# First products of the experts in seven half-size forms, and float64 weights turned to float32 beforehand

## The chip, the cores and the metric

One Trainium2 chip, one of its cores. The metric is device time in microseconds (us) of one execution. Engines: PE (TensorE, matrix products into PSUM banks), DVE (VectorE), ACT (ScalarE), POOL (GpSimd), SP (SyncE, which issues the DMAs).

## The reference, cut to what matters

An attention layer (2 batches of 768 tokens, 8 heads) gives x, 1536 tokens of 512 values. On x works a layer of eight experts, on its result a gated last layer. All is float32, but the last layer's weights and the lengths come as eight-byte numbers.

```python
logits = x @ w_gate
P = np.exp(logits - logits.max())
for _ in range(8):
    P /= P.sum(1, keepdims=True) + 1e-09
    P /= P.sum(0, keepdims=True) + 1e-09
    P *= N / E
for e in range(E):                      # 8 experts, w1[e] 512 x 1024, w2[e] 1024 x 512
    h = np.maximum(x @ w1[e], 0.0)      # the first products
    out += P[:, e:e + 1] * (h @ w2[e])  # the second products
# last layer: w_gate, w_val 512 x 1536 and w_out 1536 x 512, all float64
gate = 1.0 / (1.0 + np.exp(-(x @ w_gate)))
y = gate * (x @ w_val) @ w_out
```

## The kernel before

Matrix products run as three float32r passes on operands that are split in two parts, x = high + low: high x high, low x high, high x low (`product`, lines 283 to 285). So every operand exists twice: `xh`, `xl` (x with its 512 values on the partitions, tokens as columns), `wh`, `wl` (weights), `hh`, `hl` (the hidden layer). A split is an ACT copy for the high part and a subtraction for the low one, on POOL for weights (line 203) and on DVE for results in a bank (line 317).

The work comes in visits. A visit is a quarter of an expert (256 of its 1024 hidden values), or a sixth of the last layer, over all its chunks of tokens. `unit_first` makes the first products of a chunk: for each of 2 blocks of 128 hidden values 12 products (4 blocks of the contraction, 3 passes) into one bank, then ACT's Relu (316) and DVE's `hl` (317). `unit_second` makes the second products one unit later: per block of 128 tokens 6 products of 512 columns, which DVE adds to `acc` with the gate as factor (359). Chunks have 4 blocks of tokens (512 columns) from the second expert on. The first expert is done in two batches of 768 tokens with chunks of 3 blocks (384 columns): the first batch beside the second batch's attention, the second beside the gate. The gate's logits, then eight rounds of row and column sums (`gate_steps`), are issued step by step between the products of that second batch; a column sum is a PE product with ones (961), and a chain of eight DVE operations (lines 967 to 974 and 952 to 955) makes what the next one reads.

All queues are in the order in which the code issues (`manual_schedule`); `Paced` spreads side work over ticks, one after each product group. While a visit runs, the weights of the next are split (`split_steps`); its last step issues the load that refills the raw buffer (`load`, on SP). From the last expert visit on, each visit's next weights are float64, loaded as pairs of words and taken apart by `split_double`: seven DVE operations of 1024 columns, one on ACT, one on POOL for each of three parts. In the last layer `turn_y` transposes the experts' sum into `xh`, `xl`, paced over the last expert visit and the first of the last layer.

## Time and profile before

| | us |
|---|---|
| median of 3 runs | 1505.39 (1503.59 to 1505.69) |
| span of the profiled execution | 1504.86 |
| PE busy / DVE busy / ACT busy / POOL busy | 1485.4 / 740.1 / 346.6 / 241.0 |
| chain that ended last: PE / DVE | 95% / 3% |
| first products, 512 columns | 3 x 960 |
| first products, 384 columns | 3 x 128 |
| second products, 512 columns | 3 x 912 |

The profile is one execution of the program. Busy PE time is modelled and products overlap in it, so the distance between the starts of products tells more than their durations. Waits are inferred from semaphores; a wait that stands in a row in brackets is idle time of that row's engine just ahead of it. Lines (L283) are those of the kernel printed above.

### The profile page before, as it was taken

The page shows a single profiled execution, that of the slowest core. Times are in us where ns is not written, and L with a number is a line of the kernel's source. Part 1 is how long each engine was busy: PE and PEld are TensorE (multiplying, and loading weights), DVE is VectorE, ACT ScalarE, POOL GpSimd, SP SyncE. Part 2 cuts the span into 40 slices and gives each one's busy share as a digit, 9 for nine tenths or more (in the row PEclk, how much of TensorE's full clock was granted, in tenths as well). Part 3 has the DMA queues.
Part 4 walks back from the last instruction along what each step waited for, and adds up shares of the span by engine and source line. Part 5 has one row for each costly group of instructions (what it writes and reads, how often), then busy time and mean ns, then how long its engine had stood idle before and what let it go on. Part 6 is the DMA issues. An engine that isn't in the chain of part 4 may idle for free.

```text
span 1504.9 us, 17508 instructions
## 1 busy us (share of the span) xinstructions
PE 1485.4 (99%) x7091; PEld 1233.7 (82%) x7091; DVE 740.1 (49%) x1257; ACT 346.6 (23%) x638; POOL 241.0 (16%) x254
## 2 busy tenths in 40 slices
PE   8999998999999999999999999999999999999998
PEld 6889877888888888888888888888888788888887
DVE  5654436553443434343434444343454676786663
ACT  5754322211112111111111111111111232222121
POOL 4322102211111112111211111121211100110010
PEclk9999999999999999999999999999999999999999
DMA  8421101101000101100010100011011101211102
GB/s 192 95 69 39 29 30 56 43 28 43 29 29 29 42 29 30 41 29 28 28 43 29 42 29 28 28 36 35 30 41 57 56 28 57 84 56 57 56 0 84
DMA packets 75525, 68.30 MB, mean 45 GB/s; under 512 B 40112, under 2 KB 57520, under 8 KB 75440
## 3 DMA queue, kind: packets, MB, share of 16 engines
q1 hardware_dynamic: 75152, 67.14, 14.9%
q8 instruction: 57, 0.93, 0.3%
q14 instruction: 28, 0.23, 0.0%
q10 hardware_dynamic: 288, 0.00, 0.0%
HBM read 63.98 MB, written 3.15 MB: 45 GB/s over the span
## 4 chain that ended last, share of the span: by engine, by line
PE 95%; DVE 3%; ACT 1%; issue 1%; DMA 0%; DVEq 0%; ACTq 0%; POOL 0%; POOLq 0%
PE bank L283 30%; PE bank L285 29%; PE bank L284 29%; PE bank L652 1%; PE bank L682 1%; PE bank L700 1%; PE bank L696 1%; PE bank L507 0%; ACT e L669 0%; DVE acc L359 0%; PE bank L518 0%; DVE qT L622 0%; DMA lens<-in_n_local_dram 0%; PE bank L1003 0%; DVE e L664 0%
## 5 line engine op out<-in xcount | busy, mean ns | idle before, releaser
L283 PE MATMUL bank<-xh,wh 128*128 128x512 f32 (+1 forms) x1088 | 421.0, 387 | 2.8 <-issue 2.8
L284 PE MATMUL bank<-xl,wh 128*128 128x512 f32 (+1 forms) x1088 | 418.8, 385 | 0.3 <-DVE xl L1008 0.2
L285 PE MATMUL bank<-xh,wl 128*128 128x512 f32 (+1 forms) x1088 | 418.8, 385 | 0.0
L283 PE MATMUL bank<-wh,hh 128*128 128x512 f32 x912 | 359.5, 394 | 0.0
L285 PE MATMUL bank<-wh,hl 128*128 128x512 f32 x912 | 355.9, 390 | 0.0
L284 PE MATMUL bank<-wl,hh 128*128 128x512 f32 x912 | 355.5, 390 | 0.0
L317 DVE SCALAR_TENSOR_TENSOR hl<-bank,hh 128x512 fp32r<-128x512 f32 (+1 forms) x200 | 134.0, 670 | 432.0 <-ACT hh L316 432.0
L359 DVE SCALAR_TENSOR_TENSOR acc<-bank,gate,acc 128x512 f32<-128x512 f32 x336 | 252.1, 750 | 145.2 <-PE bank L285 140.8
L316 ACT ACTIVATE hh<-bank 128x512 fp32r<-128x512 f32 (+1 forms) x200 | 116.2, 581 | 821.9 <-PE bank L285 815.7
L203 POOL TENSOR_TENSOR wl<-raw,wh 128x512 fp32r<-128x512 f32 x136 | 174.0, 1300 | 790.1 <-ACT wh L201 788.3
L283 PEld LDWEIGHTS bank<-xh,wh 128*128 128x128 f32 x1088 | 205.2, 189 | 42.3 <-issue 3.0
L284 PEld LDWEIGHTS bank<-xl,wh 128*128 128x128 f32 x1088 | 205.5, 189 | 39.9 <-DVE xl L1008 1.2
L285 PEld LDWEIGHTS bank<-xh,wl 128*128 128x128 f32 x1088 | 205.5, 189 | 38.5
L285 PEld LDWEIGHTS bank<-wh,hl 128*128 128x128 f32 x912 | 171.3, 188 | 36.5
L283 PEld LDWEIGHTS bank<-wh,hh 128*128 128x128 f32 x912 | 171.7, 188 | 35.6
L284 PEld LDWEIGHTS bank<-wl,hh 128*128 128x128 f32 x912 | 171.5, 188 | 34.3
L274 POOL TENSOR_TENSOR wl<-raw 128x1024 fp32r<-128x1024 f32 x18 | 34.1, 1896 | 282.3 <-PE bank L285 139.7
L201 ACT ACTIVATE wh<-raw 128x512 fp32r<-128x512 f32 x136 | 78.6, 623 | 0.0
L331 DVE TENSOR_TENSOR z<-bank,sg 128x512 f32<-128x512 f32 x36 | 24.9, 690 | 66.0 <-PE bank L285 66.0
L669 ACT ACTIVATE e<-e,mn 128x256 f32<-128x256 f32 (+1 forms) x96 | 41.9, 483 | 50.0 <-DVE mn L664 49.8
L332 ACT ACTIVATE hh<-z 128x512 fp32r<-128x512 f32 x36 | 22.7, 632 | 88.0 <-DVE z L331 88.0
L333 DVE TENSOR_TENSOR hl<-z,hh 128x512 fp32r<-128x512 f32 x36 | 27.6, 768 | 25.1 <-ACT hh L332 25.1
(112 smaller groups left out, 768.7 us busy)
## 6 DMA issues: line engine op xcount, KB each, us to landing
raw<-in_moe_w_dram SPq DMA_DIRECT2D x68, 512.0 KB, 3.5
raw<-in_moe_w_val_dram SPq DMA_DIRECT2D x6, 1024.0 KB, 5.2
raw<-in_moe_w_gate_dram SPq DMA_DIRECT2D x6, 1024.0 KB, 5.2
raw<-in_moe_w_out_dram SPq DMA_DIRECT2D x6, 1024.0 KB, 4.9
out_dram<-o SPq DMA_DIRECT2D x12, 256.0 KB, 2.0
qr<-in_q_dram SPq DMA_DIRECT2D x14, 192.0 KB, 4.0
kr<-in_k_dram SPq DMA_DIRECT2D x14, 192.0 KB, 4.2
vo<-in_v_dram SPq DMA_DIRECT2D x14, 192.0 KB, 3.3
```

Source lines behind the costliest of these rows:

```text
L201: steps.append(lambda r=r, h=h: nc.scalar.activation(out=h, in_=r, func=AF.Copy))
L203: lambda r=r, h=h, lo=lo: nc.gpsimd.tensor_tensor(out=lo, in0=r, in1=h.bitcast(F32), op=ALU.subtract)
L274: nc.gpsimd.tensor_tensor(out=lo, in0=low, in1=high, op=ALU.mult)
L283: nc.tensor.matmul(out=ps, lhsT=ah, rhs=bh, start=(i == 0), stop=False)
L284: nc.tensor.matmul(out=ps, lhsT=ah, rhs=bl, start=False, stop=False)
L285: nc.tensor.matmul(out=ps, lhsT=al, rhs=bh, start=False, stop=(i == n - 1))
L316: nc.scalar.activation(out=hh[hid][:, f, :m], in_=ps, func=AF.Relu)
L317: nc.vector.scalar_tensor_tensor(out=hl[hid][:, f, :m], in0=ps, scalar=0.0, in1=hh[hid][:, f, :m].bitcast(F32), op0=ALU.max, op1=ALU.subtract,
L331: nc.vector.tensor_tensor(out=z, in0=ps, in1=sg, op=ALU.mult)
L333: nc.vector.tensor_tensor(out=hl[hid][:, f, :m], in0=z, in1=hh[hid][:, f, :m].bitcast(F32), op=ALU.subtract,)
L359: nc.vector.scalar_tensor_tensor(out=a, in0=ps, scalar=gate[:, t, e : e + 1], in1=a, op0=ALU.mult, op1=ALU.add,)
L669: nc.scalar.activation(out=e[:, j, lo:KW], in_=e[:, j, lo:KW], func=AF.Exp, scale=-1.0, bias=mn[:, j : j + 1],)
```

## The change

From the second expert on a visit is of a new kind (`fast`). Contraction (512), hidden values (256) and tokens (768 of a batch) are each cut in two halves, and the eight half-size products that make a visit's first products of one batch are replaced by seven products of combinations, by the Strassen scheme in Winograd's form. `pair` runs them for a batch: each form is 6 PE products of 384 columns; a form may add to what an earlier one left in its bank, after ACT has copied that (`copied`) and before DVE adds a copy (`summed`). One second product, or two, stands between forms.

- The weights' seven forms: four POOL operations on 256 columns (`sum_steps`) and seven splits of 256 columns on ACT and POOL (`form_step`), for the next visit beside this one. All visits share one set of forms.
- The tokens' forms: `trans_steps` makes them once per batch, 8 DVE operations and 4 splits on 768 columns, issued beside the gate (`other`). One block of `xh`, `xl` is overwritten by its form.
- The hidden layer has three buffers, not two.
- The last layer's weights: `double_steps` fetches float64 in 36 half-pieces, turns each to float32 on DVE (6 operations on 512 columns), ACT (1) and POOL (2), and stores it to DRAM (`glw`), step by step over 26 of the 28 visits. In the last layer they are loaded and split as other weights are, by ACT and POOL.
- The turning of y: the first chunk's transposes stand among the last six second products of the experts, the others in the first visit of the last layer.

```diff
+    hh3 = const.tile([P, HID, 2, C], F32R, name="hh3")
+    glw = [dram.tile([P, 4 * FQ], F32, name=f"glw{i}") for i in range(3 * NFF)]
...
-                dict(kind="moe", e=e, f=f, chunks=chunks, slot=1 - len(visits) % 2, load=True)
+            visits.append(dict(kind="fast", e=e, f=f, slot=1 - len(visits) % 2, load=True))
...
+    def split_one(r, h, lo):
+        nc.scalar.activation(out=h, in_=r, func=AF.Copy)
+        nc.gpsimd.tensor_tensor(out=lo, in0=r, in1=h.bitcast(F32), op=ALU.subtract)
...
+    def sum_steps(n):
+        a, (s1, s2, s3, s4) = w1_blocks(n), sums()
+        for out, x, y, op in (
+            (s1, a[1, 0], a[1, 1], ALU.add), (s2, s1, a[0, 0], ALU.subtract),
+            (s4, a[0, 1], s2, ALU.subtract), (s3, a[0, 0], a[1, 0], ALU.subtract),
+        ):
+            yield lambda out=out, x=x, y=y, op=op: nc.gpsimd.tensor_tensor(
+                out=out, in0=x, in1=y, op=op
+            )
+    def form_step(n, i):
+        a, (s1, s2, s3, s4) = w1_blocks(n), sums()
+        src = (a[0, 0], s1, s2, s4, s3, a[0, 1], a[1, 1])[i]
+        h, lo = form(i)
+        split_one(src, tall(h), tall(lo))
...
+        return [
+            fetch, no_tick, no_tick, rest, first_a, first_b, keep, kept, scaled, whole, no_tick,
+            store,
+        ]
...
+        run(0, x, block(0, 0))
+        copied(0, x)
+        slots(0)
+        run(1, z, trans(0))
+        copied(1, z)
+        slots(1)
+        seconds(1)
+        run(2, x, trans(1), start=False)
+        copied(2, x)
+        slots(2)
+        seconds(1)
+        run(3, z, block(1, 1), start=False)
+        summed(t_hid, 0, z, snap[:, 2])
+        slots(3)
+        seconds(1)
+        run(4, x, trans(2), start=False)
+        summed(t_hid, 1, x, snap[:, 1])
+        slots(4)
+        seconds(1)
+        run(5, y, block(1, 0))
+        o_hid = next_hid()
+        summed(o_hid, 0, y, snap[:, 0])
+        slots(5)
+        seconds(2)
+        run(6, x, block(0, 1), start=False)
+        hidden(o_hid, 1, x)
...
+        return [
+            whole(r11, 0, 0), whole(r12, 0, 1), whole(r22, 1, 1), whole(r21, 1, 0),
+            less(r11, r12, r11), put(r11, th[:, 0, :, b, :], tl[:, 0, :, b, :]),
+            less(r12, r22, r12), put(r12, th[:, 2, :, b, :], tl[:, 2, :, b, :]),
+            less(r22, r22, r11), put(r22, th[:, 1, :, b, :], tl[:, 1, :, b, :]),
+            less(r21, r21, r22), put(r21, *block(0, 1)),
+        ]
...
+    trans = [x for b in range(B) for x in trans_steps(b)]
     side = Paced(gate_steps(), 5 * CB * NQ - 2)
-    for n in range(NB0, 2 * NB0):
-        run_visit(n, side.tick)
+    other = Paced([no_tick] * 6 + trans[:-1], 5 * CB * (NQ - 1))
...
+    for n in range(NB0, F0 - 1):
+        run_visit(n, both, split_steps(n + 1))
+    other.finish()
...
+    ahead = [*sum_steps(F0), *(lambda i=i: form_step(F0, i) for i in range(4)), *second_steps(F0)]
+    run_visit(n, side.tick, ahead)
     side.finish()
+    trans[-1]()
+    for i in range(4, 7):
+        form_step(F0, i)
+    load(visits[F0]["raw"])
...
+    doubles = Paced(double_steps(), 26 * (last - F0 - 1))
```

Three places show how the queues change. The first is DVE in the gate stage, around one chain of the gate (`csum` to the second `gate` row); `acc` and `hl` are the first expert's, `work` holds the tokens' combinations. Before:

```order
L349 COPY acc_5355<-bank_68 128x512
L317 SCALAR_TENSOR_TENSOR hl_79<-bank_63,hh_77 128x384
L317 SCALAR_TENSOR_TENSOR hl_79<-bank_64,hh_77 128x384
L967 TENSOR_REDUCE csum<-bank_70 128x8
L970 TENSOR_SCALAR csum<-csum 128x8
L973 RECIPROCAL csum<-csum 128x8
L974 TENSOR_TENSOR gate<-gate,csum 128x96
L952 TENSOR_REDUCE rsum<-gate 128x12
L953 TENSOR_SCALAR rsum<-rsum 128x12
L954 RECIPROCAL rsum<-rsum 128x12
L955 TENSOR_TENSOR gate<-gate,rsum 128x96
L351 TENSOR_TENSOR acc_5355<-bank_66,acc_5355 128x512
```

In the changed kernel:

```order
L1122 TENSOR_TENSOR work<-work 128x768
L427 COPY acc_5373<-bank_68 128x512
L393 SCALAR_TENSOR_TENSOR hl_77<-bank_63,hh_76 128x384
L1122 TENSOR_TENSOR work<-work 128x768
L393 SCALAR_TENSOR_TENSOR hl_77<-bank_64,hh_76 128x384
L1204 TENSOR_REDUCE csum<-bank_70 128x8
L1207 TENSOR_SCALAR csum<-csum 128x8
L1210 RECIPROCAL csum<-csum 128x8
L1211 TENSOR_TENSOR gate<-gate,csum 128x96
L1189 TENSOR_REDUCE rsum<-gate 128x12
L1190 TENSOR_SCALAR rsum<-rsum 128x12
L1191 RECIPROCAL rsum<-rsum 128x12
```

Two combinations of 768 columns now stand ahead of the chain, and others between the next ones.

The second is SP at the load that follows the first fast visit's split; `raw` is a buffer of raw weights, `work` here the buffer of float64 words, `glw` the store in DRAM. Before:

```order
L182 DMA raw_88<-in_moe_w_dram 128x4x256
L182 DMA raw_88<-in_moe_w_dram 128x2x512
L182 DMA raw_89<-in_moe_w_dram 128x4x256
L182 DMA raw_89<-in_moe_w_dram 128x2x512
L182 DMA raw_88<-in_moe_w_dram 128x4x256
L182 DMA raw_88<-in_moe_w_dram 128x2x512
L182 DMA raw_89<-in_moe_w_dram 128x4x256
L182 DMA raw_89<-in_moe_w_dram 128x2x512
```

In the changed kernel:

```order
L175 DMA raw_86<-in_moe_w_dram 128x4x256
L175 DMA raw_86<-in_moe_w_dram 128x2x512
L297 DMA work<-in_moe_w_gate_dram 128x2x512
L340 DMA glw_90<-work 128x512
L297 DMA work<-in_moe_w_gate_dram 128x2x512
L175 DMA raw_87<-in_moe_w_dram 128x4x256
L175 DMA raw_87<-in_moe_w_dram 128x2x512
L340 DMA glw_90<-work 128x512
L297 DMA work<-in_moe_w_val_dram 128x2x512
```

The conversion's first fetch stands behind that load, and each further fetch behind the store of the one before it, with weight loads between.

The third is DVE in the expert visits, around one unit of first products before and part of one batch's forms after; `kept` holds the copies of banks and the sums. Before:

```order
L317 SCALAR_TENSOR_TENSOR hl_78<-bank_63,hh_76 128x512
L317 SCALAR_TENSOR_TENSOR hl_78<-bank_64,hh_76 128x512
L359 SCALAR_TENSOR_TENSOR acc_5355<-bank_70,gate,acc_5355 128x512
L359 SCALAR_TENSOR_TENSOR acc_5355<-bank_67,gate,acc_5355 128x512
L359 SCALAR_TENSOR_TENSOR acc_5355<-bank_68,gate,acc_5355 128x512
L359 SCALAR_TENSOR_TENSOR acc_5355<-bank_69,gate,acc_5355 128x512
L317 SCALAR_TENSOR_TENSOR hl_79<-bank_65,hh_77 128x512
L317 SCALAR_TENSOR_TENSOR hl_79<-bank_66,hh_77 128x512
L359 SCALAR_TENSOR_TENSOR acc_75<-bank_70,gate,acc_75 128x512
L359 SCALAR_TENSOR_TENSOR acc_75<-bank_67,gate,acc_75 128x512
```

In the changed kernel:

```order
L539 TENSOR_TENSOR kept<-bank_66,kept 128x384
L437 SCALAR_TENSOR_TENSOR acc_75<-bank_68,gate,acc_75 128x512
L531 SCALAR_TENSOR_TENSOR hl_77<-kept,hh_76 128x384
L301 TENSOR_SCALAR work<-work 128x512
L539 TENSOR_TENSOR kept<-bank_64,kept 128x384
L308 TENSOR_SCALAR work<-work 128x512
L437 SCALAR_TENSOR_TENSOR acc_75<-bank_69,gate,acc_75 128x512
L531 SCALAR_TENSOR_TENSOR hl_77<-kept,hh_76 128x384
L539 TENSOR_TENSOR kept<-bank_65,kept 128x384
L314 SCALAR_TENSOR_TENSOR work<-work 128x512
L437 SCALAR_TENSOR_TENSOR acc_75<-bank_70,gate,acc_75 128x512
L531 SCALAR_TENSOR_TENSOR hl_77<-kept,hh_76 128x384
```

The additions into `kept`, on which later forms wait, now stand among the second products' sums and the conversion's operations on `work`.

## Rows read from the trace of the kernel before

**Rows 1.** The page's parts 1 and 2: busy us, share, instructions; then clock by slice.

```profile
PE 1485.4 (99%) x7091; PEld 1233.7 (82%) x7091; DVE 740.1 (49%) x1257; ACT 346.6 (23%) x638; POOL 241.0 (16%) x254
...
PEclk9999999999999999999999999999999999999999
```

**Rows 2.** The page's part 4: the chain that ended last, share of the span by engine.

```profile
PE 95%; DVE 3%; ACT 1%; issue 1%; DMA 0%; DVEq 0%; ACTq 0%; POOL 0%; POOLq 0%
```

**Rows 3.** Busy us of each engine by window (instructions), granted clock, DMA share, GB/s.

```profile
220.00:272.00 52.00, 47.35 (x229) 42.57 (x228) 31.51 (x82) 9.60 (x19) 10.68 (x9) 0.93 0.13 41
280.00:1180.00 900.00, 900.00 (x3972) 745.25 (x3971) 378.96 (x521) 157.32 (x276) 140.15 (x109) 1.00 0.10 33
```

**Rows 4.** PE in order of time: start us, us, line, operation, out<-in, shape.

```profile
379.91 0.39 PE L283 MATMUL bank<-wh,hh 128*128 128x512 f32 x1
...
383.76 0.39 PE L285 MATMUL bank<-wh,hl 128*128 128x512 f32 x1
```

**Rows 5.** PE in order of time, 384 columns.

```profile
247.12 0.33 PE L283 MATMUL bank<-xh,wh 128*128 128x384 f32 x1
...
248.19 0.33 PE L283 MATMUL bank<-xh,wh 128*128 128x384 f32 x1
...
251.14 0.33 PE L285 MATMUL bank<-xh,wl 128*128 128x384 f32 x1
```

**Rows 6.** DVE by line and shape: out<-in, count, busy us, mean ns, idle before, releaser.

```profile
L359 DVE SCALAR_TENSOR_TENSOR acc<-bank,gate,acc 128x512 f32<-128x512 f32 x336 | 252.1, 750 | 145.2 <-PE bank L285 140.8
...
L333 DVE TENSOR_TENSOR hl<-z,hh 128x512 fp32r<-128x512 f32 x36 | 27.6, 768 | 25.1 <-ACT hh L332 25.1
...
L253 DVE SCALAR_TENSOR_TENSOR tmp<-raw,tmp 128x1024 int32<-128x1024 int32 x18 | 22.0, 1222 | 0.4
...
L317 DVE SCALAR_TENSOR_TENSOR hl<-bank,hh 128x384 fp32r<-128x384 f32 x32 | 17.8, 558 | 56.1 <-ACT hh L316 56.1
```

**Rows 7.** ACT and POOL by line and shape, the whole span.

```profile
L316 ACT ACTIVATE hh<-bank 128x384 fp32r<-128x384 f32 x32 | 15.7, 492 | 75.9 <-PE bank L285 69.8 <-DVE rsum L953 6.0
...
L203 POOL TENSOR_TENSOR wl<-raw,wh 128x512 fp32r<-128x512 f32 x136 | 174.0, 1300 | 790.1 <-ACT wh L201 788.3 <-issue 1.0 <-DVE qT L622 0.7
...
L606 POOL TENSOR_TENSOR bm<-bm,msk 128x256 f32<-128x256 f32 x6 | 4.4, 726 | 0.2
```

**Rows 8.** The page's part 6: DMA issues, KB each, us to landing.

```profile
raw<-in_moe_w_dram SPq DMA_DIRECT2D x68, 512.0 KB, 3.5
raw<-in_moe_w_val_dram SPq DMA_DIRECT2D x6, 1024.0 KB, 5.2
```

**Rows 9.** PE in order of time around a wait of the gate stage.

```profile
257.59 0.46 PE L961 MATMUL bank<-gate,ones 128*128 128x96 f32 x2 [1.78 <-DVE gate L955]
...
259.49 0.52 PE L285 MATMUL bank<-xh,wl 128*128 128x384 f32 x1
...
262.05 0.52 PE L284 MATMUL bank<-xl,wh 128*128 128x384 f32 x1
```

**Rows 10.** DVE in order of time: two chains of the gate stage.

```profile
246.57 0.25 DVE L967 TENSOR_REDUCE csum<-bank 128x8 f32<-128x96 f32 x1
...
246.85 0.17 DVE L970 TENSOR_SCALAR csum<-csum 128x8 f32<-128x8 f32 x1
...
248.34 0.26 DVE L955 TENSOR_TENSOR gate<-gate,rsum 128x96 f32<-128x96 f32 x1
...
254.01 1.15 DVE L970 TENSOR_SCALAR csum<-csum 128x8 f32<-128x8 f32 x1
```

**Rows 11.** DVE by line, 220 to 272 us.

```profile
L974 DVE TENSOR_TENSOR gate<-gate,csum 128x96 f32<-128x96 f32 x7 | 3.4, 482 | 0.2
...
L970 DVE TENSOR_SCALAR csum<-csum 128x8 f32<-128x8 f32 x7 | 3.2, 457 | 0.2
...
L953 DVE TENSOR_SCALAR rsum<-rsum 128x12 f32<-128x12 f32 x7 | 1.9, 266 | 0.2
```

**Rows 12.** Waits from 1150 to 1200 us: us in total, times, longest.

```profile
PE bank L1003 <- DVE xl L1008: 1.5, 2, 1.2
```

More of the change, by code (lines that the diff above doesn't have):

```diff
@@ L25 @@
 FILL = 4
-HID = 2
+HID = 3
 PACE = 13
@@ L187, in load, with piece, load_piece, split_halves @@
             )
+    def piece(i):
+        return raw[i // 2 % 2][:, i % 2 * 4 * FQ : (i % 2 + 1) * 4 * FQ]
+    def load_piece(i):
+        if i < 3 * NFF:
+            nc.sync.dma_start(out=piece(i), in_=glw[i])
+    def split_one(r, h, lo):
+        nc.scalar.activation(out=h, in_=r, func=AF.Copy)
+        nc.gpsimd.tensor_tensor(out=lo, in0=r, in1=h.bitcast(F32), op=ALU.subtract)
+    def split_halves(r, h, lo):
+        for half in range(2):
+            cols = slice(half * 2 * FQ, (half + 1) * 2 * FQ)
+            yield lambda cols=cols: split_one(r[:, cols], h[:, cols], lo[:, cols])
+    def second_steps(n):
+        vis = visits[n]
+        r = raw[vis["raw"]][:, 4 * FQ : 8 * FQ]
+        yield from split_halves(r, wh[vis["slot"]][1], wl[vis["slot"]][1])
     def split_steps(n):
-        if n >= len(visits) or not visits[n]["load"]:
-            return []
         vis = visits[n]
@@ L380, in turn, with run_visit @@
             turns.pop(0)[1]()
-    def run_visit(n, tick, after=None):
+    def run_visit(n, tick, ahead):
         chunks = visits[n]["chunks"]
-        steps = split_steps(n + 1)
         per = chunks[0][1] + (2 if visits[n]["kind"] == "moe" else 4)
-        ahead = Paced(steps, per * (len(chunks) - 1) * (12 if n == last else PACE) // 12)
+        ahead = Paced(ahead, per * (len(chunks) - 1) * PACE // 12)
         side = tick
@@ new lines, in run_fast, with before, after @@
+    def run_fast(n, side):
+        fast = n < last
+        ahead = list(sum_steps(n + 1)) if fast else []
+        seconds = list(second_steps(n + 1)) if fast else []
+        def before(i):
+            side()
+            if i is None and ahead:
+                ahead.pop(0)()
+        def after(i):
+            side()
+            if not fast:
+                if i is not None:
+                    state["after"](i)
+            elif i is None:
+                if seconds:
+                    seconds.pop(0)()
+            elif i > 0:
+                form_step(n + 1, i - 1)
+        pair(n, 0, before)
+        for step in ahead:
+            step()
+        pair(n, 1, after)
+        if fast:
+            form_step(n + 1, 6)
+            load(visits[n + 1]["raw"])
```

440 lines of the change are left out of this document (275 added, 165 removed).

## The prediction

> **What bounds the kernel now.** The page's first parts come first: PE is busy for 1485.4 of 1504.9 us, its granted clock is full in every slice, DVE and POOL for 49% and 16% [rows 1]. The chain that ended last is 95% PE [rows 2]. So a PE product that is removed shortens the span, and added work on another engine costs only where PE waits for it. Two windows show both kinds of place. From 280 to 1180 us (the experts from the second on) PE never idles; from 220 to 272 us (the gate's normalisation, beside the first expert's second batch) PE is busy for 47.35 of 52 us at a mean clock of 0.93 [rows 3].
>
> PE's busy time is modelled, so products are priced by the distance between their starts. Eighteen 512-column products in a row start from 379.91 to 383.76 us: 3.85 / 17 = 226.5 ns each [rows 4]. Eighteen 384-column ones start from 248.19 to 251.14 us: 2.95 / 17 = 173.5 ns [rows 5]. That is 0.766 for 0.75 of the columns: about 13 ns of each product don't shrink.
>
> **First products: the term that pays.** A visit (a quarter of an expert, 28 of them from the second expert on) has 3 chunks of 2 blocks with 12 first products each, 72 of 512 columns: 72 x 0.2265 = 16.31 us. Changed, it has 2 batches of 7 forms with 6 products each, 84 of 384 columns: 84 x 0.1735 = 14.57 us. The gain is 1.74 us a visit, 28 x 1.74 = 48.6 us. By columns alone (one eighth less) it would be 28 x 2.04 = 57 us; the fixed 13 ns of 336 additional products take the rest. The stretch of 24 that follows a change of width gives 174.8 ns (247.12 to 251.14) [rows 5], hence 45.6 us; I take 48, with 45 as its lower bound. PE gets no other work: its instruction list is longer by exactly these 336 products with their loads.
>
> Section "Wait — 56ns, not 53.3ns?" of the Trainium skill's page "TensorE: Matmul & The Clock Gate" puts the start-to-start distance at columns by 2.4 GHz plus about 2.5 ns. By that the gain would be 28 x (72 x 215.8 - 84 x 162.5 ns) = 53 us, an estimate from the page; the trace has larger fixed parts, so the rows decide.
>
> **The seven forms' other work in a visit pair.** A pair (one batch) lasts 42 x 0.1735 + 36 x 0.2265 = 15.4 us on PE. DVE gets 6 sums into `acc` at 0.75, 3 additions and 4 `hl` at 0.56, and 0.69 of a float64 half-piece (36 in 26 visits; six operations of at most 0.61, half of the dearest 1024-column row): 4.5 + 3.9 + 2.5 = 10.9 us. ACT gets 7 copies or Relus at 0.49 and not as much again for forms: under 7 us. POOL gets 2 sums and 3.5 forms at 0.73, one half at 1.30 and the conversion's two operations at 1.30: 7.1 us [rows 6, 7]. All fit in 15.4.
>
> In order, too, there is room. Form 2 accumulates on the bank that ACT copied after form 0: between them lie form 1 and one second product, 1.04 + 1.36 = 2.4 us, for a 0.49 us copy. Form 6 needs DVE's addition of form 4: form 5 and two second products lie between, 3.8 us, for 0.56. I cost steady pairs at nothing; PE's own second products cover them. A float64 fetch that comes behind two weight loads on SP can hold DVE up: three transfers of 512 KB land after about 3.5 + 2 x (5.2 - 3.5) = 6.9 us [rows 8], and the operation that waits is placed some 6 us after its fetch. This falls on about six of 36 fetches, mostly inside the slack: +1 us, bounds 0 and 8.
>
> **First fast visit.** Here the load that SP must issue ahead of the first fetch waits for POOL, which has 4 sums and 7 forms (8.0 us), two halves (2.6) and one 768-column subtraction (about 1.95, 1.5 x 1.30) to do, 12.6 us from about where the last chunk begins, 8.3 us ahead of the visit [rows 7]. So the load is issued 4.3 us into the pair and the fetch lands near 11.2. DVE waits for it with the addition of form 4 queued behind. This pair has only three second products pending, so PE reaches form 6 at 6 x 1.04 + 3 x 1.36 = 10.3 us and gets its bank at about 12.3. A wait of 1.78 us in the trace is followed by products 0.32 us apart, that is the clock's lower level of 1.2 GHz, for some 3.2 us before they are back at 0.17; that costs another 1.5 us [rows 9]. I take 2.0 + 1.5 = +3.5 us, bounds 0 and 6.
>
> **Gate stage: the term that costs.** Between the gate's sums the changed kernel places DVE's 16 operations on 768 columns that make the token combinations, 14 of them from 220 us on. Their nearest rows are 768 ns (512 columns, two SBUF inputs) and 1222 ns (1024) [rows 6]: about 1.0 us each. DVE is busy for 31.5 of 52 us there now, but in order: the gate's chain lasts 2.0 us (246.57 to 248.60), stands in DVE's queue behind the stage's `hl` and `acc`, and PE's next sum waits for it, visibly so already [rows 3, 9, 10].
>
> POOL's work collides besides. A step of the chain that meets a weight split takes 1.15 us, 0.17 alone [rows 10]. Over the seven chains of the window the three steps that suffer average 457, 266 and 482 ns [rows 11], where the first two take 0.17 us alone and the third's like 0.26 [rows 10]: 0.61 us a chain, 4.3 us for the window's nine POOL operations [rows 3], 0.47 each. Seven more, half as long again: 7 x 0.7 = 4.9 us. The 14 new DVE operations meet POOL too: busy (10.7 + 13.7) of some 55 us, 44%, half an operation's wait of 0.8 us: 14 x 0.35 = 4.9 us. DVE then has 31.5 + 14 + 4.9 + 4.9 = 55 us of work. With 8% of unavoidable waiting on top the stage takes 60 us for 52: **+8 us**. Bounds: 0, if all of it vanishes in DVE's 20.5 idle us, and +24, if none does. I take the value at which DVE is nearly full, since each of seven chains makes PE wait for DVE's queue.
>
> Section "SBUF: two separate sides" of the Trainium skill's page "SBUF — State Buffer" says that a DVE operation in a two-port mode or with two SBUF inputs, and a GpSimd operation, exclude each other for a whole instruction. The trace agrees: a step of the chain grew by 0.98 us [rows 10], less than one POOL split of 1.30. Were every such wait as long as a POOL operation, the stage would come to the upper bound of the sum above, which is rival C.
>
> **Last layer.** Its products stay. DVE loses the float64 splitting, ACT and POOL get six halves per visit, at 1.30 us on POOL [rows 7], beside 3 x 72 products of 0.2265, 49 us. The turning of the first chunk moves among six second products; PE's 1.5 us of waiting for `xl` there [rows 12] may go: -1.5 us, bounds -2 and +4. Earlier stages keep their order but for a split whose two halves are issued together: 0.
>
> **Sum**, against the profiled execution: 1504.9 - 48 + 8 + 3.5 + 1 - 1.5 = 1467.9. The median of the runs shown stands 0.5 above the span: **1468 us**.
>
> **Rivals.** A is the sum above. B, all the added work is hidden: the gate stage and the first pair at their lower bounds, 1504.9 - 48.6 - 2 + 0.5 = 1455 us. For it speaks that DVE idles 40% of the gate window; against it that the chains leave it no free order.
>
> C, DVE and POOL get in each other's way: +24 in the gate stage, +6 in the first pair, +8 by late fetches, 1504.9 - 45 + 24 + 6 + 8 = 1498 at the worst, 1485 in the middle. For it speak the steps of 1.15 us; against, the 0.47 us that a POOL operation cost on average.
>
> D, on the other side: PE waits in every pair. The place is form 6, which waits for DVE's addition behind a DVE queue that POOL holds up. A pair with 15.4 us of PE work replaces 16.3, so it decides at 0.87 us of waiting in each. DVE has 10.9 us of work in 15.4, and some seven operations per pair (3 `hl`, 4 of the conversion) that POOL can hold for at most 1.3 us each, 9.1 us: with the whole of it a pair is bound by DVE at 20.0 us and the kernel ends near 1505 + 56 x 3.7 = 1712; with 6.4 us, at 17.3, near 1561. Against it stands that the point where it decides, 16.3 us, asks for a mean wait of (16.3 - 10.9) / 7 = 0.77 us, where 0.47 was measured.
>
> E, the change doesn't do what it says: narrower products alternate with wide ones and keep the wide ones' pace. At 0.194 us each the gain is gone (72 x 0.2265 / 84), 1505 us or more with the gate's cost. Against it speaks [rows 5], where they run at 0.1735 right behind wide ones.
>
> **How the numbers follow.** Chances: A 0.52 (1461 to 1478), B 0.17, C 0.22, D 0.05, E 0.04. The predicted time is A's, 1468. The range takes A, B and C's middle: from 1454 (B) to 1487 us, leaving out C's upper part, D and E. A measurement tells some 0.2% (3 us) from no change: faster by more than that 0.92 (A, B, C but for its very end), within it 0.03 (part of C and E), slower 0.05 (D, part of E).
>
> **What the next profile would show.** Starts of the forms' products 0.173 to 0.178 us apart, and PE at full clock through the pairs: the first term. A gate window with DVE above 90% busy, gate sums that wait for DVE at four or more of seven places, and clock slices below 1: the second. One PE wait of about 2 us at form 6 of the first fast pair. The forecast is wrong if waits for DVE or ACT repeat pair by pair in the fast visits, if the forms' starts lie at 0.19 us or more, or if the gate stage is as long as before.

## The result, and the profile after

The changed kernel takes **1490.84 us** (median of 4 runs, 1484.2 to 1494.34) beside 1505.54 us for the kernel before: a ratio of 0.990 (0.987 to 0.993). The forecast was 1468 us (1454 to 1487). The direction was right and the size was not: 15 us were won, where 37 were forecast. The runs of the changed kernel also lie 10 us apart; those of the kernel before lie within 3.3.

From the page of the changed kernel (busy time of each engine; then shares in 40 slices; then the chain that ended last), beside [rows 1] and [rows 2]:

```profile
PE 1465.4 (98%) x7427; PEld 1282.4 (86%) x7427; DVE 859.7 (58%) x1587; ACT 499.6 (33%) x1064; POOL 523.9 (35%) x604
PE   8999998899999999999999999999999999999998
DVE  4455437867666657666666666667665533333323
POOL 3312103454444444445345445344452211121110
PEclk8799999999999999999999999999999999999999
PE 95%; DVE 2%; POOL 1%; issue 1%; ACT 1%; DMA 1%; SPq 0%; DVEq 0%; ACTq 0%; POOLq 0%
```

PE has 20 us less work by this count where 48 were forecast, and its clock is no longer full in the first two slices. The windows of the changed kernel (columns as in [rows 3]: stretch, length, busy time and count of each engine, PE's clock, DMA) say where:

```profile
20.00:40.00 20.00, 19.08 (x103) 17.26 (x103) 8.29 (x35) 10.32 (x24) 10.53 (x20) 0.58 0.52 108
60.00:80.00 20.00, 19.54 (x108) 17.86 (x108) 8.10 (x31) 9.03 (x21) 2.90 (x10) 0.57 0.21 60
206.00:298.00 92.00, 82.19 (x390) 70.69 (x391) 63.45 (x124) 24.67 (x47) 31.57 (x25) 0.93 0.08 24
312.00:1150.00 838.00, 837.88 (x4178) 755.86 (x4179) 564.42 (x923) 294.84 (x656) 383.83 (x419) 1.00 0.20 68
```

The same two stretches of the attention in the kernel before:

```profile
20.00:40.00 20.00, 19.25 (x169) 16.91 (x168) 12.14 (x50) 14.82 (x34) 10.46 (x21) 1.00 0.72 150
60.00:80.00 20.00, 19.19 (x168) 16.57 (x164) 12.59 (x50) 13.79 (x33) 2.86 (x11) 1.00 0.70 167
```

PE looks equally busy in them, but gets through 103 instructions and not 169: it runs at the lower of its two clocks (1.2 GHz) for most of both. That is in the attention, where the forecast had put zero. In the pairs of the fast visits (312 to 1150 us) PE never idles and the clock is full, as forecast; but the products stand further apart than they were priced. By stage, with borders at the first product behind the attention, the first form of the fast visits and the first product of the last layer (the kernel before has four second products, 5.4 us, behind the last border; they are counted ahead of it here):

| stage, us | before | after | measured | forecast |
|---|---|---|---|---|
| attention | 191.2 | 206.1 | +14.9 | 0 |
| gate stage | 85.3 | 92.1 | +6.8 | +8 |
| experts from the second on, turning included | 921.7 | 885.8 | -35.9 | -45 |
| last layer | 306.6 | 307.9 | +1.3 | 0 |
| sum (spans 1504.9 and 1492.0) | | | -12.9 | -37 |

(The forecast's -1.5 us for the turning stands in the third line, with -48, +3.5 and +1.) So there are two misses: 14.9 us in the attention, and some 10 in the products' distances.

**The attention.** Three extracts of the changed kernel's timeline around 58 us (start, length, engine, line, operation; in brackets the idle time before it and what ended it). On ACT:

```profile
56.59 0.91 ACT L870 ACTIVATE e<-e,mn 128x256 f32<-128x256 f32 x2 [0.48 <-DVE mn L865]
57.40 0.61 ACT L191 ACTIVATE wh<-raw 128x512 fp32r<-128x512 f32 x1
```

On POOL:

```profile
55.39 0.24 POOL L859 CAST kT<-kT 128x64 fp32r<-128x64 f32 x1 [1.24 <-PE bank L853]
58.10 1.27 POOL L192 TENSOR_TENSOR wl<-raw,wh 128x512 fp32r<-128x512 f32 x1 [2.47 <-ACT wh L191]
```

And on PE:

```profile
57.75 0.66 PE L883 MATMUL bank<-ident,e 128*128 128x128 f32 x4
60.46 0.44 PE L897 MATMUL bank<-vo,aT 128*128 128x65 f32 x2 [2.06 <-POOL vo L906]
```

POOL takes its instructions in order. The subtraction that makes `wl` was issued in one step with ScalarE's copy, and ScalarE reached that copy only behind two Exps, at 57.40. POOL stood still for 2.47 us and then needed 1.27 more, and the small copy into `vo` that PE's next product reads was queued behind. PE waited 2.06 us, and then ran at half its clock until some 78 us: the windows 65 to 70 and 70 to 75 us have a clock of 0.50. A smaller wait, of 0.70 us for POOL's copy into `kT`, stands at 22.7 us, ahead of the first such stretch (23 to 40 us).

**The distances.** Rows of PE in a steady pair of the changed kernel, first products of each form and first of each block of second products:

```profile
507.05 0.34 PE L354 MATMUL bank<-xh,wh 128*128 128x384 f32 x1
508.12 0.39 PE L354 MATMUL bank<-wh,hh 128*128 128x512 f32 x1
509.51 0.34 PE L354 MATMUL bank<-th,wh 128*128 128x384 f32 x1
...
1254.43 0.40 PE L354 MATMUL bank<-xh,wgh 128*128 128x512 f32 x1
...
1260.03 0.40 PE L354 MATMUL bank<-wh,hh 128*128 128x512 f32 x1
```

Six products of 384 columns take 1.07 us here, 178 ns each, where [rows 5] gave 173.5; six of 512 take 1.39 us, 232 ns each, where [rows 4] gave 226.5. In the last layer (the last two rows, 24 products apart) it is 5.60 / 24 = 233 ns, with no change of width at all.

### The profile page after: what moved, and what is told of

Same layout as the page of the kernel before. It is cut to its first block, busy times and chain, and to the rows that moved or that the text cites. A ratio compares the mean times of both kernels' runs of the same rounds, so it can differ in the third digit from the quotient of the medians.

```text
span 1492.0 us, 19772 instructions
## 1 busy us (share of the span) xinstructions
PE 1465.4 (98%) x7427; PEld 1282.4 (86%) x7427; DVE 859.7 (58%) x1587; ACT 499.6 (33%) x1064; POOL 523.9 (35%) x604
## 4 chain that ended last, share of the span: by engine, by line
PE 95%; DVE 2%; POOL 1%; issue 1%; ACT 1%; DMA 1%; SPq 0%; DVEq 0%; ACTq 0%; POOLq 0%
PE bank L354 29%; PE bank L356 29%; PE bank L355 29%; PE bank L853 2%; PE bank L901 1%; PE bank L883 1%; PE bank L897 1%; PE bank L708 1%; POOL wl L192 0%; PE bank L719 0%; DMA work<-in_moe_w_gate_dram 0%; PE bank L1282 0%; DMA lens<-in_n_local_dram 0%; DVE work L1122 0%; DVE csum L1207 0%
## 5 line engine op out<-in xcount | busy, mean ns | idle before, releaser
L192 POOL TENSOR_TENSOR wl<-raw,wh 128x512 fp32r<-128x512 f32 (+1 forms) x188 | 201.8, 1089 | 378.4 <-ACT wh L191 370.3
L354 PE MATMUL bank<-xh,wh 128*128 128x384 f32 (+1 forms) x720 | 255.5, 355 | 5.4 <-DVE kept L539 3.0
L356 PE MATMUL bank<-xh,wl 128*128 128x384 f32 (+1 forms) x720 | 252.9, 351 | 0.0
L355 PE MATMUL bank<-xl,wh 128*128 128x384 f32 (+1 forms) x720 | 251.7, 350 | 0.0
L529 ACT ACTIVATE hh<-kept 128x384 fp32r<-128x384 f32 x168 | 88.1, 525 | 314.5 <-DVE kept L539 314.5
L192 POOL TENSOR_TENSOR wl<-work,wh 128x256 fp32r<-128x256 f32 x112 | 93.4, 835 | 94.3 <-ACT wh L191 94.3
L531 DVE SCALAR_TENSOR_TENSOR hl<-kept,hh 128x384 fp32r<-128x384 f32 x168 | 115.3, 687 | 0.4 <-ACT hh L529 0.3
L356 PE MATMUL bank<-th,wl 128*128 128x384 f32 x336 | 113.0, 336 | 0.0
L354 PE MATMUL bank<-th,wh 128*128 128x384 f32 x336 | 112.5, 335 | 0.1
L355 PE MATMUL bank<-tl,wh 128*128 128x384 f32 x336 | 112.4, 335 | 0.0
```

The costliest lines, as they stand in the source:

```text
L192: nc.gpsimd.tensor_tensor(out=lo, in0=r, in1=h.bitcast(F32), op=ALU.subtract)
L354: nc.tensor.matmul(lhsT=ah, rhs=bh, start=first, stop=False, **mm)
L355: nc.tensor.matmul(lhsT=ah, rhs=bl, start=False, stop=False, **mm)
L356: nc.tensor.matmul(lhsT=al, rhs=bh, start=False, stop=end, **mm)
L529: nc.scalar.activation(out=hh[:, f, :C], in_=src, func=AF.Relu)
L531: lambda: nc.vector.scalar_tensor_tensor(out=hl[:, f, :C], in0=src, scalar=0.0, in1=hh[:, f, :C].bitcast(F32), op0=ALU.max, op1=ALU.subtract,)
```

## The experiments

The distances in this table, in ns, are means between the starts of neighbouring products (those under 300 ns, so without waits), over 330 to 1150 us for the fast visits and over 1210 to 1450 us for the last layer; "attention ends" and the gate stage, in us, are of the one profiled execution and bordered as above.

| kernel | median us | attention ends | gate stage | 512 / 384 columns, fast | last layer |
|---|---|---|---|---|---|
| before | 1505.5 | 191.2 | 85.3 | 226.7 / - | 229.9 |
| after | 1490.8 | 206.1 | 92.1 | 230.2 / 175.3 | 231.3 |
| e1_split_apart | 1479.6 | 190.9 | 91.3 | 230.2 / 175.2 | 231.6 |
| e2_grouped | 1480.3 | 190.9 | 92.3 | 228.3 / 174.6 | 231.6 |
| e3_before_joined | 1515.2 | 200.1 | - | 226.7 / - | 230.0 |
| e4_phase | 1472.2 | 190.7 | 89.4 | 231.1 / 174.3 | 226.7 |
| e5_early | 1464.3 | 190.6 | 88.0 | 231.0 / 174.4 | 226.7 |
| e6_grouped_early | 1464.3 | 190.7 | 88.0 | 228.9 / 174.8 | 226.7 |
| g1_no_low | 1464.9 | 190.9 | 86.4 | - | - |
| g2_no_combinations | 1459.8 | 190.6 | 81.3 | - | - |
| g3_dense | 1464.7 | 190.6 | 87.6 | - | - |

**e1_split_apart: the halves of a split in steps of their own.** In `split_steps`:

```
-                steps += split_halves(r, wh[...][0], wl[...][0])
-                steps += second_steps(n)
+                for j in range(2):
+                    for half in range(2):
+                        ...
+                        steps.append(lambda r=r, h=h: nc.scalar.activation(out=h, in_=r, func=AF.Copy))
+                        steps.append(lambda r=r, h=h, lo=lo: nc.gpsimd.tensor_tensor(...))
```

> The changed kernel, but in the first expert's visits the ScalarE copy and the GpSimd subtraction of each weight split are steps of their own again, as in the kernel before. Theory J (joined halves): in the changed kernel the subtraction goes onto GpSimd's queue together with the copy that it needs, so GpSimd stands still until ScalarE gets to that copy (2.47 us at 58.10 us), the small vo and kT copies that PE needs stand behind it, PE waits 2.06 us and then runs for some 16 us at half its clock; twice in the profiled execution, 14.9 us. J expects the end of the attention stage back near 191 us (206 in the changed kernel), no stretch at half clock in it, a median near 1476 us (1472 to 1480), and runs that lie within some 3 us of each other (10 us in the changed kernel). Rival M (another memory layout or another order elsewhere causes the low-clock stretches): still one or two stretches at half clock, 1484 to 1494 us.

Measured: 1479.63 us (1479.0 to 1480.11), 0.983 of before (0.982 to 0.985); the attention ends at 190.9 us. Its windows:

```profile
20.00:40.00 20.00, 19.34 (x168) 17.02 (x168) 12.14 (x50) 14.67 (x34) 10.30 (x21) 1.00 0.71 140
60.00:80.00 20.00, 19.20 (x165) 16.52 (x162) 12.59 (x50) 13.78 (x33) 2.84 (x11) 1.00 0.72 170
```

Full clock, and nearly the counts of the kernel before. The five runs lie 1.1 us apart, where those of the changed kernel lay 10, with mean clocks from 0.983 to 0.993: how much of a run PE spent at half clock differed, and with the waits the spread goes. Theory J holds.

**e3_before_joined: the same step joined in the kernel before,** in its `split_steps`, for the first expert only:

```
+                    def both_halves(r=r, h=h, lo=lo):
+                        nc.scalar.activation(out=h, in_=r, func=AF.Copy)
+                        nc.gpsimd.tensor_tensor(out=lo, in0=r, in1=h.bitcast(F32), op=ALU.subtract)
+                    if vis["e"] == 0:
+                        steps.append(both_halves)
+                        continue
```

> The kernel before, with the copy and the subtraction of each weight split of the first expert issued in one step, as the changed kernel does; nothing else. Theory J: stretches at half clock appear in the attention stage here too, the stage ends 8 to 16 us later in most executions, median 1511 to 1522 us with a spread of some 8 us. Rival M: as the kernel before, 1505 us, within 2 us.

Measured: 1515.18 us (1511.48 to 1517.06), 1.0065 of before (1.0052 to 1.0078). PE's longest wait in its attention (total, times, longest):

```profile
PE bank L705 <- POOL vo L714: 2.5, 2, 2.0
```

Two of its windows:

```profile
40.00:60.00 20.00, 17.39 (x131) 15.28 (x130) 10.38 (x42) 12.76 (x30) 9.44 (x18) 0.88 0.29 60
60.00:80.00 20.00, 20.00 (x135) 18.08 (x135) 9.76 (x39) 10.50 (x25) 2.60 (x10) 0.70 0.47 113
```

The same wait of 2.0 us for `vo` and one low stretch: 0.65%, 9.8 us, without anything else of the change. The cause is shown from both sides. Its PE waits 0.70 us for `kT` at 22.7 us too, as in the changed kernel, but keeps the full clock there (1.00 from 20 to 40 us): not every such wait is followed by a low stretch.

**e2_grouped: fewer changes of width in a pair.** On the base of e1, in `pair`:

```
-        seconds(1)
+        early = len(pending) // 2
+        seconds(early)
         run(2, x, trans(1), start=False)
...
-        seconds(2)
+        seconds(6 - early)
```

with the three `seconds(1)` behind forms 2 to 4 taken out.

> As e1_split_apart, and in each pair of the fast visits the second products stand in two groups of three (after form 1 and after form 5), not 1, 1, 1, 1, 2. So a pair has 4 changes between 384 and 512 columns and not 10. Theory W (a change of width costs): the products right after a change start irregularly, 224 to 236 ns apart where 226.6 is the settled distance of 512 columns and 169 to 185 where 173.5 is that of 384, and lose some 20 ns in all at each change. W expects the means 230.1 and 175.3 ns to come down, by more than half of their excess (below 228.5 and 174.5), 0.1 us a pair, 5 to 7 us in all against e1_split_apart. Rival P (addresses: th, tl and the weights of the last layer lie at another phase of 256 bytes than all other operands): means as they are, time as e1_split_apart within 1.5 us. PE may wait about 1 us more at form 6 of the first pair, which has only three second products to place.

Measured: 1480.29 us, the time of e1, as rival P had it. But the means came down, as theory W has it: to 228.3 ns (expected below 228.5) and 174.6 (just short of 174.5), 42 x 0.6 + 36 x 1.8 ns = 91 ns a pair, 5.1 us. The gain went into new waits. From the list of PE's waits (total, times, longest):

```profile
PE bank L362 <- ACT kept L551: 6.4, 4, 3.7
```

One of them, of 3.7 us, ends at 540.8 us. DVE just ahead of it:

```profile
539.30 0.43 DVE L309 TENSOR_SCALAR work<-work 128x512 int32<-128x512 int32 x1 [3.46 <-DMA work<-in_moe_w_out_dram]
```

and ACT:

```profile
539.76 0.65 ACT L312 ACTIVATE work<-work 128x512 f32<-128x512 int32 x1 [8.21 <-DVE work L309]
540.32 0.47 ACT L551 ACTIVATE kept<-bank 128x384 f32<-128x384 f32 x1
```

A float64 fetch stood behind two weight loads; DVE waited for it, ScalarE's next conversion step for DVE, and ScalarE's copy of form 0, which form 2 needs, behind that step. This is the late fetch of the forecast. In the changed kernel it is hidden, because second products lie between the forms.

**e4_phase: 192 bytes of padding.** On the base of e1:

```
+    pad = late.tile([P, 48], F32, name="pad")
+    nc.vector.memset(pad[:, 0:1], 0.0)
     moe = ExitStack()
```

> As e1_split_apart, with 192 bytes of padding per partition ahead of the buffers of the fast visits and of the last layer, so that all operands of PE start at the same phase of 256 bytes (128); in the changed kernel th, tl, the gate and value weights and the last layer's hidden buffers start at 192. Theory P (addresses): all products settle at 226.6 and 173.5 ns, 11 us less in the fast visits and up to 6 less in the last layer against e1_split_apart. Theory W (changes of width): the fast visits stay at 230.1 and 175.3 ns; the last layer, where every product has 512 columns, may come down from 231.6 if it has a cause of its own in the addresses.

Measured: 1472.15 us (1470.78 to 1475.35), 7.5 less than e1. In the last layer all products stand 226.7 ns apart: the 24 products between these rows take 5.45 us, where they took 5.60.

```profile
1236.38 0.39 PE L362 MATMUL bank<-xh,wgh 128*128 128x512 f32 x1
...
1241.83 0.39 PE L362 MATMUL bank<-wh,hh 128*128 128x512 f32 x1
```

The last layer is 5.8 us shorter. In the fast visits the products of 384 columns come 0.9 ns closer together and those of 512 move as far apart, which neither theory had: next to nothing in sum (886.8 us, 887.6 in e1). So in the fast visits the cost is W's, in the last layer P's. The changed kernel's last layer shows P by operand too: products on the new buffers `wgh` and `wvh`, or on the last layer's hidden buffers, stand 233.3 ns apart, those of `xh` with the older `wh` 227. The kernel before has a mean of 229.9 there, so e4's layer is faster than that one as well; whether addresses are the cause there was not tried.

The gate stage came out 1.9 us shorter, and most of that is not the padding's. Ahead of its first product PE waits 2.6 us in e1 and 2.3 in e4; then e1 runs at half clock and e4 does not. From 190 to 195 us, e1 and then e4:

```profile
190.00:195.00 5.00, 4.07 (x14) 4.07 (x15) 0.00 (x0) 0.23 (x1) 0.00 (x0) 0.66 0.02 7
190.00:195.00 5.00, 4.35 (x25) 4.35 (x26) 0.62 (x2) 0.49 (x1) 0.00 (x0) 1.00 0.02 7
```

The stage's first 24 products take 5.84 us in e1 and 4.27 in e4. The kernel before, the changed one, e2, e6, g1 and g2 have this low stretch as well, e3, e5 and g3 do not; there are kernels with the padding and without it among both. So 1.4 to 1.6 us of a difference between two gate stages of the table can be this alone.

**m1_distances: the cost by itself.** Nothing but products, each kind on a line of its own:

```
for i, w in enumerate(same(512, 0, 16)):      # 48 products; weights 16 floats further
    nc.tensor.matmul(**put(i, w))
for i, w in enumerate(turns(6, (512, 0, 0), (384, 0, 0))):   # 6 and 6, 144 in all
    nc.tensor.matmul(**put(i, w))
```

> The disputed cost by itself: only TensorE products of zeros (the output is left at zero, nothing of the reference is computed), every one with its own 128x128 weights, 48 or 72 in a row of each kind, nothing else on the core. Kinds: 512, 384 and 256 columns with both operands at the same phase of 256 bytes; 512 and 384 columns with the weights or the moving operand 64 bytes (16 floats) further, or both, and the weights 32, 128 and 192 bytes further; 512 and 384 columns in turns of 1, 3, 6, 12, 18 and 36; 512 columns with the operands' phases changing every 6 or 12. Theory W+P: both effects exist and are TensorE's own. Settled distance 226.6 and 173.4 ns where the phases agree and the width stays; some 231 to 233 ns for 512 columns where weights and moving operand differ by 64 bytes (231.6 in the last layer of the changed kernel), 226.6 again when both are moved; turns of 6 some 20 ns dearer per change of width than the settled distances, turns of 36 the same 20 ns per change and so hardly visible. Rival: the longer distances come from other engines' accesses to SBUF or from the waits that products carry; then all kinds here lie at 226.6 and 173.4.

Its timeline on PE, one row a kind (L87 to L91: 512, 384 and 256 columns; L93, L95, L97: 512 with the weights, the moving operand, both 64 bytes further; L99: the weights 128 bytes). A kind's distance is the next row's start less its own, by the count:

```profile
34.23 11.04 PE L87 MATMUL bank<-mv,st 128*128 128x512 f32 x48
45.11 8.51 PE L89 MATMUL bank<-mv,st 128*128 128x384 f32 x48
53.45 5.91 PE L91 MATMUL bank<-mv,st 128*128 128x256 f32 x48
59.20 11.37 PE L93 MATMUL bank<-mv,st 128*128 128x512 f32 x48
70.40 11.16 PE L95 MATMUL bank<-mv,st 128*128 128x512 f32 x48
81.40 11.06 PE L97 MATMUL bank<-mv,st 128*128 128x512 f32 x48
92.30 11.30 PE L99 MATMUL bank<-mv,st 128*128 128x512 f32 x48
```

And the turns of both widths, of 6 (L109), 12 (L111), 36 (L115), 3 (L117) and 1 (L119), and of two phases (L121):

```profile
142.33 29.37 PE L109 MATMUL bank<-mv,st 128*128 128x512 f32 x144
171.53 29.36 PE L111 MATMUL bank<-mv,st 128*128 128x512 f32 x144
...
229.80 29.09 PE L115 MATMUL bank<-mv,st 128*128 128x512 f32 x144
258.73 29.52 PE L117 MATMUL bank<-mv,st 128*128 128x512 f32 x144
288.09 29.91 PE L119 MATMUL bank<-mv,st 128*128 128x512 f32 x144
317.84 33.46 PE L121 MATMUL bank<-mv,st 128*128 128x512 f32 x144
```

With both operands at one phase, 512, 384 and 256 columns stand 226.7, 173.7 and 119.8 ns apart (rows L87, L89, L91). Weights 64 bytes further: 11.20 / 48 = 233.3 ns (L93). The moving operand 64 bytes further: 229.2 (L95), the weights 128 bytes: 232.1. Both 64 bytes further: 227.1, and 226.7 once settled (L97). 144 products of both widths would take 72 x 226.7 + 72 x 173.3 ns = 28.80 us at the settled distances. In turns of 6 they take 29.20 (L109), 0.40 more for 24 changes, 17 ns a change; in turns of 36 28.93 (L115), 33 ns for each of 4; in turns of 1 29.75 (L119), 7 ns for each of 144. The single starts after a change to 512 columns are 229, 233, 236, 224, 231, 236, 228, 233 and 231 ns apart and then 226.7 for good; behind a change to 384 they are 171, 175, 178, 185, 176 and 181, then 173.3. That is 41 and 26 ns lost. In turns of six, from the second pair of turns on, they are the first six of the wide row (29 ns lost) and 172, 179, 173, 174, 173 and 173 (4 ns). The blocks of six in e4's pairs show both rows of six, to a nanosecond; in the changed kernel, with its other phases, only one wide block of six in four does. In turns of six of two phases (L121) 144 products take 33.30 us, 0.5 more than at the settled distances of both phases. No other engine runs here and nothing waits: both effects come about on TensorE alone, and the rival falls.

**e5_early: the combinations and the conversion earlier.** On the base of e4:

```
-    other = Paced([no_tick] * 6 + trans[:-1], 5 * CB * (NQ - 1))
+    other = Paced(trans[:-1], 4 * CB * (NQ - 1))
-    doubles = Paced(double_steps(), 26 * (last - F0 - 1))
+    doubles = Paced(double_steps(), 26 * (last - F0 - 1) - 6)
-        run_fast(n, doubles.tick)
+        run_fast(n, doubles.tick if n > F0 else no_tick)
```

> As e4_phase, with the 23 steps of the token combinations started at once and paced over 24 ticks (before: after 6 empty steps, over 30), and the float64 conversion started one visit later. Theory of the gate stage (the combinations' DVE operations and their 1.85 us GpSimd subtractions stretch the gate's chains, of which two now make PE wait 4.5 and 4.7 us): the stage (89.4 us in e4_phase, 85.3 in the kernel before) loses one of the two waits or both with their half-clock stretches, 4 to 6 us less. Theory of the first pair (the wait of 3.2 us at form 6 comes from DVE waiting for a float64 fetch): the wait goes, with 1 us of half clock behind it, 4 us less. Together 1462 to 1465 us. Rival: the waits only move to other chains and to the next visit's first pair, 1470 to 1473 us.

Measured: 1464.27 us (1462.69 to 1464.71), ratio 0.973 (0.972 to 0.974): 26.6 us below the changed kernel. The wait of the first pair is gone and the fast visits are 5.1 us shorter (881.7): that theory holds. The gate stage lost 1.5 us and not 4 to 6: there the waits moved, as the rival had it. It still has four waits for the gate:

```profile
PE bank L1208 <- DVE gate L1202: 8.1, 4, 3.3
```

**g1_no_low and g2_no_combinations: what the gate stage pays for.** In `trans_steps`, on the base of e4:

```
         def put(r, h, lo):
-            return lambda: split_one(r, h, lo)
+            def step():
+                nc.scalar.activation(out=h, in_=r, func=AF.Copy)
+                nc.scalar.activation(out=lo, in_=r, func=AF.Copy)
+            return step
```

and in g2_no_combinations `whole` is a ScalarE copy and `less` is empty besides.

> As e4_phase (gate stage 89.4 us from the first product behind the attention to the first form, 85.3 in the kernel before), but the low half of each token combination is written by a ScalarE copy and not by GpSimd's subtraction (wrong values, for the time alone); DVE's 16 operations stay. Theory L (lock): the 1.85 us subtractions on GpSimd hold single steps of the gate's chain (1.77 us for a step of 0.26), so without them PE's two waits of 4.5 and 4.7 us shrink to the 1.8 and 2.9 us of the kernel before and the stage to 86 us or less. Theory Q (queue): DVE's 0.95 us operations ahead of the chains make them late; the stage stays at 88 to 89 us.

> As g1_no_low, and DVE's 16 operations for the combinations are left out too (ScalarE copies of the high halves stand in their place, wrong values, for the time alone). Both theories: the stage at 85 to 86 us. If it stays above 87, the rest of the cost comes from GpSimd's sums and forms in the last visit of the stage. The difference between this and g1_no_low is the price of DVE's share.

Measured: the stage is 86.4 us without the low halves and 81.3 without the combinations, beside 89.4. By these differences POOL's eight subtractions cost 3.0 us, DVE's 16 operations 5.1. But g1 and g2 have the low stretch at the stage's start (its first 24 products take 5.62 and 5.85 us), which e4 has not; without it POOL's share would be some 4.4 us. How POOL's share comes about, e4's DVE at the first of the two waits:

```profile
230.87 0.20 DVE L1220 RECIPROCAL csum<-csum 128x8 f32<-128x8 f32 x1
231.10 1.77 DVE L1221 TENSOR_TENSOR gate<-gate,csum 128x96 f32<-128x96 f32 x1
```

and its POOL:

```profile
230.95 1.81 POOL L192 TENSOR_TENSOR tl<-work,th 128x768 fp32r<-128x768 f32 x1 [1.77 <-ACT th L191]
```

A step of 0.26 us takes 1.77, until POOL's instruction ends at 232.76. PE's waits for the gate in e4:

```profile
PE bank L1208 <- DVE gate L1202: 9.2, 2, 4.7
```

in g1:

```profile
PE bank L1212 <- DVE gate L1206: 5.7, 2, 3.6
```

and in g2:

```profile
PE bank L1210 <- DVE gate L1204: 3.5, 2, 2.2
```

Theory L has 3.5 of the 9.2 us of waiting, theory Q another 2.2: both hold in part. That g2 comes out 4 us *below* the kernel before was expected by neither. Both issue the same 391 products there; but the kernel before waits 4.7 us for the gate and g2 3.5, and the kernel before runs at half clock behind both waits (a mean of 0.66 from 235 to 240 and from 258 to 263 us), g2 behind neither (1.00 from 230 to 240 and from 250 to 260 us). So a part of what the combinations cost, 6.8 us from before to after and 8.1 from e4 to g2, is the clock's.

g1 shows one thing more: its first fast pair waits 1.3 us at form 6, where e4 waits 3.2. POOL, without the subtraction of 1.87 us that stands among its forms, is done 4.3 us into the pair and not 6.1, as in the changed kernel.

**e6_grouped_early and g3_dense: two attempts at a better kernel.** e6 is e5 with e2's groups and with each fetch issued right behind the last reader of its buffer:

```
+        for steps, follow in zip(halves, halves[1:] + [[no_tick]]):
+            yield from steps[3:9]
+            yield follow[0]      # the next fetch
+            yield steps[9]
...
```

> As e5_early, with the second products in two groups of three as in e2_grouped, and each float64 fetch issued right after the last reader of its buffer, 5 steps ahead of the operation that waits for it (2 before). In e2_grouped the distances fell as expected (91 ns a pair, 5.1 us) but PE waited 6.4 us for ScalarE's copies of form 0, behind the conversion's fetch that came after two weight loads (6.4 us to land). Theory: with the earlier fetch these waits go and the 5 us stay: 1457 to 1460 us. Rival: without second products between forms 2 to 5 PE waits for the copies in any case, time as e5_early or above.

Measured: 1464.33 us. The waits for ScalarE's copies fell from 6.4 to 0.3 us, but by the distances the grouping is worth only 59 ns a pair here, 3.3 us, and of these 1.7 went at the end, where the turning waits for the last sums, and 0.9 in the pairs between. Time as e5: the expected 1457 to 1460 did not come.

g3 is e6 with `Paced(trans[:-1], 11)` and the last pair ungrouped.

> As e6_grouped_early, with the combinations' 23 steps paced over 11 ticks (24 there), so that they are done before the Sinkhorn chains begin, and the last pair of the last visit in the ungrouped order. Theory: the stage comes to 86 us (88.0), the turn's wait of 1.1 us at the end goes: 1460 to 1462 us. Rival: DVE, full in the first visit of the stage, makes PE wait for its hidden operands there: no gain, 1464 us or more.

Measured: 1464.67 us (1460.97 to 1466.51). The turning's wait went; the gate stage came to 87.6 us and not to 86, since PE waits 2.0 us for DVE in its first visit instead. The rival is right in the time and the engine; what PE waits for is the gate's maximum (`gmx`), not the hidden operands. The medians of e5, e6 and g3 can't be told apart; e5_early does it with the smallest edit.

## Why the prediction was off

**"Earlier stages keep their order but for a split whose two halves are issued together: 0"** is the step that failed most: 14.9 us in the profiled execution, 11.2 in the medians (e1 against after). The difference was seen and left unpriced. The question to be asked of it was the one that the forecast asked of DVE's queue: what is queued behind the instruction that now waits, and who waits for that. POOL's small copies for `kT` and `vo` were, and PE for these.

**First products, -48 us.** This is the second step that failed. Right in its mechanism, wrong in a size: 37.6 us by the distances (144 x 226.67 ns x 28 visits before; 56 pairs of 42 x 175.31 + 36 x 230.16 ns after). The forecast took both settled distances from long runs of one width, while a pair changes its width ten times. The sign was in its own rows: the stretch behind a change had 174.8 and not 173.5 ns [rows 5]. It was used as a bound for the narrow products; that the wide ones would pay after each change too, and more, was not asked. At the settled distances the gain would have been 49.3 us. m1 accounts for nearly all of the 11.7 that are missing: a pair has wide blocks of 6, 6, 6, 6 and 12 and narrow ones of 6, 6, 6, 6 and 18, which by m1 lose 4 x 29 + 41 + 4 x 4 + 26 = 199 ns, 11.1 us in 56 pairs. It is rival E in small: the narrow products alternate with wide ones, and both lose some of their pace.

**Gate stage, +8 us.** 6.8 measured, and 8.1 by taking the combinations away (e4 to g2). The size is right by luck, for the model behind it was wrong: DVE is not full (63.45 of 92 us), and PE waits at two sums (9.5 us) and not at four or more. The price is paid where a chain of short steps meets one of the long operations, on POOL or in DVE's own queue. In section "SBUF: two separate sides" of the Trainium skill's page "SBUF — State Buffer" a DVE operation with two SBUF inputs and a GpSimd operation that reads SBUF exclude each other for whole instructions; e4's step of 1.77 us on `gate` and `csum`, beside POOL's 1.81, agrees.

**First fast visit, +3.5 us.** Right in its mechanism: DVE waits for the float64 fetch, and form 6 for DVE's addition behind it.

```profile
310.94 0.43 DVE L301 TENSOR_SCALAR work<-work 128x512 int32<-128x512 int32 x1 [2.96 <-DMA work<-in_moe_w_gate_dram]
...
311.89 0.44 PE L354 MATMUL bank<-xh,wh 128*128 128x384 f32 x1 [3.01 <-DVE kept L539]
```

The wait is 3.0 us and not 2.0, but the clock stays full behind it (1.00 from 307 to 316 us) and the 1.5 us for it did not come: 3.2 in all, two errors that cancel. In e1 and e4 a wait of 3.6 and 3.2 us is followed by products 0.32 us apart, 5.4 and 5.0 us in all. The wait is longer because POOL stood idle for 7.2 us of the time in which the forecast had it at work: its forms wait for ScalarE's copies, and these stand behind Relus. So it is done 6.1 us into the pair and not 4.3. That e5, with the conversion started later, has no wait agrees.

**Steady pairs 0, late fetches +1 us.** No wait between 312 and 1150 us. Right within 1 us, as long as second products stand between the forms (e2).

**Last layer, -1.5 us.** The turning gained 2.1 us (3.6 before, 1.5 after), but the layer's products stand further apart than in the kernel before (231.3 and 229.9 ns), +1.3 us: the gate and value weights and the hidden buffers were allocated 64 bytes off the phase of their partners. m1's 233.3 ns for such an offset agrees with theirs, and with e4's padding the cost is gone. No term had the addresses in it.

Together: -37.6 + 14.9 + 6.8 + 3.2 + 0 - 0.8 = -13.5 us; -12.9 lie between the two spans.

The time lies near rival C's worst case (1498), but for other reasons. The rule of section "Wait — 56ns, not 53.3ns?" in the Trainium skill's page "TensorE: Matmul & The Clock Gate" (columns by 2.4 GHz and about 2.5 ns) would have put the gain at 53 us. Here the settled distance is 13.3 ns above columns by 2.4 GHz at all three widths (226.7 - 213.3, 173.3 - 160, 120.0 - 106.7), and the measurement decides.

## What to carry to other kernels

When two instructions of a pair move into one step, ask of the second engine's queue what stands behind it, even far from the change: a wait of 2 us cost some 9 through PE's clock (e3). Price products by distances taken in the order in which they will stand; a change of width costs each time, and so does an operand that starts elsewhere than its partner. A long operation on GpSimd is cheap until it meets a chain of short steps on VectorE. Before a difference between two profiled stages is given a cause, compare their granted clocks.

## What the runs showed of the hardware

- float32r products with 128x128 weights of their own stand 13.3 ns further apart than their columns at 2.4 GHz, at 256, 384 and 512 columns alike.
- After a change of width the distances swing for six to nine products before they settle: 41 ns lost in all behind a change to 512 columns, some 26 behind one to 384, where the width stays for long enough; in turns of six it is 29 and 4 (m1_distances). Why is open.
- Distances depend on how far the starts of weights and moving operand lie apart: with weights 64, 128 or 192 bytes further, 512 columns take 233.3, 232.1 and 229 ns, where steps of 512 bytes from one product's weights to the next cost nothing (m1_distances). Whether 256 bytes are the period was not tried. With 384 columns it is 174.7 ns for weights 64 bytes further and nothing for the moving operand.
- PE stayed at half its clock for some 17 us after the wait of 2.06 us in the attention, but for about 3 us after the 1.78 us of [rows 9] in the gate stage. Ahead of the gate stage a wait of 2.6 us is followed by such a stretch in e1, and one of 2.3 us by none in e4. What makes the difference was not tried.
